# Early FFN part after the attention: slots over four PSUM banks, output tiles over the tail's four, copies over four SBUF tiles

## The chip, the cores and the metric

The kernel runs on one core of a Trainium2 chip. The metric is device time in microseconds (us) of one execution; lower is better. Engines are named as in the profile: PE (TensorE matmuls), PEld (its weight loads), DVE (VectorE), ACT (ScalarE), POOL (GpSimd), SP (SyncE, which here issues all DMAs).

## What is computed

A causal attention with a compressive memory, whose output goes through a feed-forward net (FFN) with a mish-like gate. From the reference, shortened:

```python
def _attn_ref(q, k, v, M_prev, z_prev, beta):      # B, H, S, D = 4, 8, 576, 64
    a = softmax(causal(q @ k.T / sqrt(D)))
    local = a @ v
    q_p = where(q > 0, q, exp(q) - 1) + 1
    mem_out = (q_p @ M_prev) / (q_p . z_prev + 1e-6)
    g = 1 / (1 + exp(-beta))
    return g * mem_out + (1 - g) * local

def _moe_ref(x, w_in, w_out):                      # x: 2304 x 512, w_in: 512 x 2048, w_out: 2048 x 512
    h = x @ w_in
    g = h * tanh(log1p(exp(h)))
    return g @ w_out
```

The token rows x of the FFN are the attention's output: 4 sequences of 576 tokens, 8 heads of 64 columns. The FFN's weights come as 64-bit floats.

## The kernel before, in words

**Attention.** 16 pairs of heads, one after another; pair p is head pair c = p % 4 of sequence b = p // 4. For each pair: scores on PE (L364), minimum and mask on DVE (L374), exp on ACT (L381), norms on POOL (L93), transposes on PE into the banks t (L445) with copies to `at` by ACT and DVE in turn (L110, L112), products with v in two halves into the bank vps (L473). Each half is copied to `xo` by ACT, and the rest `xl` is formed by DVE. `put` (L486, L487) stores both to `xs[b]` in DRAM. So chunk c of the FFN's x, 128 of its 512 columns, is complete for a sequence when pair 4b + c has been stored.

**FFN.** Both matmuls run in three products (high by high, high by low, low by high parts of both operands). Weights are split into these parts on the chip by `narrow` (L148): a load of 512 KB into one of two buffers `raw` (L152, SP's queue), then `wa` on ACT (L91), several steps on DVE, a cast on ACT (L110). Tokens form five blocks of 512 (the last has 256). The 2048 inner columns are 16 tiles f of 128. The first six (`KA`) are the *early part*: for each block j, `load_x` (L205) loads x, four chunks of 512 KB with the two parts i = 0, 1 in loads of their own; six *slots* (`slot_a`) each accumulate 12 matmuls (4 chunks c by 3 products) into one PSUM bank, and `mish` makes g from it: ACT reads the bank and writes u (L217), ACT casts u to the high part of g (L110), DVE forms the low part (L87). Then for each 128 tokens `out_a` accumulates 18 matmuls into an *output tile* acc (L246), ACT copies it to `ob` (L110), and SP stores it to `part` in DRAM (L253).

The steps of the early part are spread over the attention, 2.4 per pair from pair 4 on. After the 16 pairs 25 steps are left: the last slot and four output tiles of block 2, all of blocks 3 and 4. `tail` runs them merged with the conversion of seven of the ten other weight tiles f. Then the tail's own loop does f = 6 to 15 for all five blocks: `mm_h` (12 matmuls into h, h3 or acc, L566) and, three units later, `mm_o` (L583) into the accumulators o0 to o3, with `part` reloaded (L581, tiles pp) and added at the end (L589).

**Banks.** PSUM has eight. The attention's pools take five (two s, two t, one v) and, once its first pairs are done, the pools ps_h (tag h, two banks) and ps_a (tag acc, one). The tail closes these and opens its own: h twice, acc, o0 to o3, h3. A slot of the early part takes the next h; an output tile takes acc for even t and the next h for odd t; all copies `ob` share one SBUF tile.

**Order.** Each engine works through one queue in order. That order is fixed when the program is built: the framework's scheduler interleaves the code's operations by their dependencies, the buffers that are free and priorities given in the code (`run`, L62; the tail's conversions are merged with the steps by `merged`, L54).

Of the kernel before, what the change touches and what calls it, by code (L numbers as in the profile page):

```python
# [8 lines left out]
F32 = mybir.dt.float32  # L9
# [9 lines left out]
NT, DM, DFF = B * S, H * D, 2048  # L19
# [42 lines left out]
def run(ops, name=None):  # L62
    off = OFF.get(name, 0)
    if off:
        with TC[0].high_priority(off):
            for op in ops:
                op()
    else:
        for op in ops:
            op()  # L70
# [6 lines left out]
def attention_moe_kernel(ctx: ExitStack, tc: tile.TileContext, f_src, qn, vn, zz, beta, w_in, w_out, out):  # L77
# [19 lines left out]
    def order_after(ins, first):  # L97
        tc.add_manual_dep(
            ins.ins, first.ins.name,
            mybir.DependencyInfo(mybir.DependencyClass.NoSync, mybir.DependencyReason.DATA), reason="order",  # L100
        )
# [6 lines left out]
    def copy(which, o, i):  # L108
        if which == "a":
            nc.scalar.copy(out=o, in_=i)  # L110
        elif which == "v":
            nc.vector.tensor_copy(out=o, in_=i)  # L112
        else:
            nc.gpsimd.tensor_scalar(out=o, in0=i, scalar1=1.0, scalar2=1.0, op0=ALU.mult, op1=ALU.mult)
# [5 lines left out]
    cp = ctx.enter_context(tc.tile_pool(name="cp", bufs=2))  # L120
    gp = ctx.enter_context(tc.tile_pool(name="gp", bufs=GPB))
    pool_of = {}

    def open_banks(st):
        pool_of["h"] = st.enter_context(tc.tile_pool(name="ps_h", bufs=2, space=PS))
        pool_of["a"] = st.enter_context(tc.tile_pool(name="ps_a", bufs=1, space=PS))

    xs = [dram.tile([128, 2, NC, S], F32, name=f"xs{b}") for b in range(B)]
    part = dram.tile([NT, DM], F32, name="part")
# [55 lines left out]
    def split(pool, own, f):  # L185
        flat = lambda t: t.rearrange("p c j -> p (c j)")
        return (narrow(pool, own, w_in[:, f], flat(wi[0, f]), flat(wi[1, f]))
                + narrow(pool, own, w_out[:, f], wo[0, f], wo[1, f]))
# [37 lines left out]

    def slot_a(j, f):
        x, n = X[j], BLOCKS[j][1]
        ps = pool_of["h"].tile([128, 512], F32, tag="h", name="h")[:, :n]
        q = 0  # L230
        for c in range(NC):
            for y, z in ((0, 0), (0, 1), (1, 0)):
                ins = nc.tensor.matmul(ps, wi[y, f][:, c, :], x[c][:, z], start=(q == 0), stop=(q == 11))  # L233
                if q == 0 and f == 0:
                    order_after(ins, before[0])
                q += 1
        d = T[j, f] = {"h": ps, "n": n, "ph": ""}
        run(mish(d))

    def out_a(j, t):  # L240
        pool, tag = (("a", "acc"), ("h", "h"))[t % 2]
        acc = pool_of[pool].tile([128, DM], F32, tag=tag, name="acc")
        for f in range(KA):
            g = T[j, f]["g"]
            for y, z in ((0, 0), (1, 0), (0, 1)):
                nc.tensor.matmul(  # L246
                    acc[:], g[:, y, 128 * t:128 * t + 128], wo[z, f],
                    start=(f == 0 and y == z), stop=(f == KA - 1 and z == 1),
                )
        o = cp.tile([128, DM], F32, tag="ob", name="ob", bufs=1)  # L250
        copy("a", o[:], acc[:])
        r0 = BLOCKS[j][0] + 128 * t
        nc.sync.dma_start(out=part[r0:r0 + 128, :], in_=o[:])  # L253
# [279 lines left out]
    def tail(mlist):  # L533
        st = ExitStack()
        open_banks(st)
        wst = st.enter_context(tc.tile_pool(name="wst2", bufs=1))
        for f in range(KA, NF):
            weights(st.enter_context(tc.tile_pool(name=f"wb{f}", bufs=1)), f, f + 1)
        pp = st.enter_context(tc.tile_pool(name="pp", bufs=4))
        ps_o = st.enter_context(tc.tile_pool(name="ps_o", bufs=1, space=PS))  # L540
        ps_i = st.enter_context(tc.tile_pool(name="ps_i", bufs=1, space=PS))
        conv = [split(wst, wst, f) for f in range(KA, NF)]
        cl = [op for x in conv[:NCV] for op in x]
        conv = conv[NCV:]
        run(merged(mlist, cl))

        blocks = [(t, min(512, NT - t)) for t in range(0, NT, 512)]
        units = [(j, f) for j in range(len(blocks)) for f in range(KA, NF)]
        nu = len(units)
        D_ = {}  # L550
        XB = {}
        P_ = {}

        def mm_h(u):
            j, f = units[u]
            t0, n = blocks[j]
            if j not in XB:
                XB[j] = load_x(t0, n)
            x = XB[j]
            pool, tag = ((pool_of["h"], "h"), (pool_of["h"], "h"), (ps_i, "h3"), (pool_of["a"], "acc"))[u % 4]  # L560
            ps = pool.tile([128, 512], F32, tag=tag, name="h")
            T["b", u] = {"h": ps[:, :n], "n": n, "ph": "T"}
            k = 0
            for c in range(NC):
                for a, b in ((0, 0), (0, 1), (1, 0)):
                    nc.tensor.matmul(  # L566
                        ps[:, :n], wi[a, f][:, c, :], x[c][:, b], start=(k == 0), stop=(k == 11)
                    )
                    k += 1
            if f == NF - 1 and j + 1 < len(blocks):  # L570
                XB[j + 1] = load_x(*blocks[j + 1])

        def mm_o(u, t):
            j, f = units[u]
            t0, n = blocks[j]
            g = T["b", u]["g"]
            if f == KA:
                D_[t] = ps_o.tile([128, DM], F32, tag=f"o{t}", name="o")
            if f == NF - 2:
                P_[j, t] = pp.tile([128, DM], F32, tag="pp", name="pp")  # L580
                nc.sync.dma_start(out=P_[j, t][:], in_=part[t0 + 128 * t:t0 + 128 * t + 128, :])  # L581
            for y, z in ((0, 0), (1, 0), (0, 1)):
                nc.tensor.matmul(  # L583
                    D_[t][:], g[:, y, 128 * t:128 * t + 128], wo[z, f],
                    start=(f == KA and y == z), stop=(f == NF - 1 and z == 1),
                )
            if f == NF - 1:
                o = P_[j, t]
                nc.vector.tensor_tensor(out=o[:], in0=D_[t][:], in1=o[:], op=ALU.add)  # L589
                nc.sync.dma_start(out=out[t0 + 128 * t:t0 + 128 * t + 128, :], in_=o[:])  # L590

        for u in range(nu + LAG):
            if u < nu:
                mm_h(u)
                d = T["b", u]
                run(mish(d))
            if conv:
                run(conv.pop(0), 'convT')
            if 0 <= u - LAG < nu:
                for t in range(blocks[units[u - LAG][0]][1] // 128):  # L600
                    mm_o(u - LAG, t)
        st.close()

    attention()
    for k in range((NP - P0) // 4, len(BLOCKS)):
        todo.extend(steps_a(k))
    tail(todo)


# [60 lines left out]
```

## Time and profile before

| | us |
|---|---|
| median of 3 runs | 655.2 (653.29 to 656.19) |
| profiled execution | 654.77 |
| its span in the trace | 653.0 |
| PE busy | 597.0 (91%), 3200 matmuls |
| PEld busy | 454.9 (70%) |
| DVE busy | 336.8 (52%) |
| ACT busy | 300.7 (46%) |
| POOL busy | 169.1 (26%) |
| DMA | 80.83 MB, mean 124 GB/s |
| mean granted PE clock | 0.973 of full |

Times in the profile count from the span's start. A row of the timeline merges neighbouring instructions of one line; what stands in brackets at its end is how long the engine was idle before it and which instruction ended that wait. A clock of 1.00 is full speed.

### The profile page before, as it was taken

The page shows a single profiled execution, that of the slowest core. Times are in us where ns is not written, and L with a number is a line of the kernel's source. Part 1 is how long each engine was busy: PE and PEld are TensorE (multiplying, and loading weights), DVE is VectorE, ACT ScalarE, POOL GpSimd, SP SyncE. Part 2 cuts the span into 40 slices and gives each one's busy share as a digit, 9 for nine tenths or more (in the row PEclk, how much of TensorE's full clock was granted, in tenths as well). Part 3 has the DMA queues.
Part 4 walks back from the last instruction along what each step waited for, and adds up shares of the span by engine and source line. Part 5 has one row for each costly group of instructions (what it writes and reads, how often), then busy time and mean ns, then how long its engine had stood idle before and what let it go on. Part 6 is the DMA issues. An engine that isn't in the chain of part 4 may idle for free.

```text
span 653.0 us, 9308 instructions
## 1 busy us (share of the span) xinstructions
PE 597.0 (91%) x3200; PEld 454.9 (70%) x3200; DVE 336.8 (52%) x903; ACT 300.7 (46%) x694; POOL 169.1 (26%) x260
## 2 busy tenths in 40 slices
PE   3477968889989999999998979999999999999997
PEld 2254635656655766767776878888888888888886
DVE  4989897765588654573338887920311211121121
ACT  3677655866567675566325455621222222222221
POOL 3697886464166714443000000000000000000000
PEclk9979986899999999999999989999999999999999
DMA  6345674324275226421257765304302220430220
GB/s 229 104 144 182 189 262 150 133 61 144 76 235 168 98 62 176 166 73 58 91 176 235 261 206 176 121 1 129 130 0 82 94 83 6 124 129 0 65 97 33
DMA packets 47007, 80.83 MB, mean 124 GB/s; under 512 B 7280, under 2 KB 21616, under 8 KB 46960
## 3 DMA queue, kind: packets, MB, share of 16 engines
q1 hardware_dynamic: 46960, 80.24, 38.0%
q8 instruction: 25, 0.41, 0.3%
q14 instruction: 22, 0.18, 0.1%
HBM read 61.35 MB, written 18.87 MB: 123 GB/s over the span
## 4 chain that ended last, share of the span: by engine, by line
PE 61%; DVE 13%; DMA 10%; ACT 7%; POOL 5%; issue 2%; SPq 1%; DVEq 0%; ACTq 0%; POOLq 0%
PE o L583 19%; PE h L566 19%; PE acc L246 7%; PE h L233 5%; DMA raw<-in_w_in_dram 5%; PE vps L473 5%; PE t L445 4%; DVE w L374 3%; PE s L364 3%; POOL w L93 3%; DMA raw<-in_w_out_dram 3%; DMA qn<-in_qn_dram 2%; ACT w L381 2%; ACT L217 1%; DVE ws L172 1%
## 5 line engine op out<-in xcount | busy, mean ns | idle before, releaser
L87 DVE TENSOR_TENSOR g<-u,g 128x512 fp32r<-128x512 f32 (+1 forms) x80 | 52.4, 661 | 185.6 <-ACT g L110 185.6
L566 PE MATMUL h<-xb,wi 128*128 128x512 f32 (+1 forms) x600 | 134.9, 368 | 0.0
L583 PE MATMUL o<-wo,g 128*128 128x512 f32 x540 | 133.8, 390 | 0.0
L217 ACT ACTIVATE u<-h 128x512 f32<-128x512 f32 (+1 forms) x80 | 43.5, 554 | 179.2 <-PE h L566 170.9
L566 PEld LDWEIGHTS h<-xb,wi 128*128 128x128 f32 x600 | 106.1, 188 | 19.6
L583 PEld LDWEIGHTS o<-wo,g 128*128 128x128 f32 x540 | 100.6, 188 | 20.3
L93 POOL TENSOR_SCALAR w<-w,rc 128x64 f32<-128x64 f32 (+4 forms) x160 | 95.4, 621 | 71.0 <-ACT w L381 53.3
L381 ACT ACTIVATE w<-w,mx 128x576 f32<-128x576 f32 (+4 forms) x160 | 88.3, 554 | 28.5 <-DVE mx L374 27.6
L364 PE MATMUL s<-f 64*128 64x288 f32 (+4 forms) x384 | 69.2, 472 | 31.7 <-DVE mx L374 25.4
L233 PE MATMUL h<-xb,wi 128*128 128x512 f32 (+1 forms) x360 | 88.0, 389 | 7.8 <-ACT u L217 7.8
L246 PE MATMUL acc<-wo,g 128*128 128x512 f32 x324 | 85.9, 401 | 1.4 <-ACT ob L110 0.9
L445 PE MATMUL t<-ident,w 128*128 128x128 f32 x480 | 75.5, 291 | 5.3 <-ACT at L110 3.1
L233 PEld LDWEIGHTS h<-xb,wi 128*128 128x128 f32 x360 | 64.8, 200 | 21.1 <-ACT u L217 9.6
L364 PEld LDWEIGHTS s<-f 64*128 64x128 f32 x384 | 35.4, 207 | 59.0 <-DVE mx L374 33.2
L445 PEld LDWEIGHTS t<-ident,w 128*128 128x128 f32 x480 | 55.9, 146 | 26.0 <-issue 8.7
L246 PEld LDWEIGHTS acc<-wo,g 128*128 128x128 f32 x324 | 59.4, 190 | 16.0 <-issue 2.3
L374 DVE CUSTOM_DVE_ANT_0 w<-s,mask 128x288 f32<-128x288 f32 (+4 forms) x160 | 59.6, 421 | 17.6 <-PE s L364 17.6
L473 PE MATMUL vps<-at,v 128*64 128x256 f32 (+2 forms) x512 | 61.3, 383 | 5.8 <-DVE xl L87 3.7
L473 PEld LDWEIGHTS vps<-at,v 128*64 128x64 f32 x512 | 35.6, 142 | 31.7 <-issue 6.0
L112 DVE COPY at<-t 128x448 f32<-128x448 f32 x64 | 41.5, 649 | 16.2 <-PE t L445 16.2
L110 ACT CAST g<-u 128x512 fp32r<-128x512 f32 (+1 forms) x80 | 45.5, 579 | 1.8
L110 ACT COPY at<-t 128x384 f32<-128x384 f32 x64 | 33.7, 526 | 17.6 <-PE t L445 17.4
(45 smaller groups left out, 432.1 us busy)
## 6 DMA issues: line engine op xcount, KB each, us to landing
f<-in_f_src_dram SPq DMA_DIRECT2D x32, 288.0 KB, 3.7
raw<-in_w_in_dram SPq DMA_DIRECT2D x16, 512.0 KB, 3.9
raw<-in_w_out_dram SPq DMA_DIRECT2D x16, 512.0 KB, 3.5
xb<-xs SPq DMA_DIRECT2D x24, 256.0 KB, 3.7
qn<-in_qn_dram SPq DMA_DIRECT2D x16, 320.0 KB, 3.4
v<-in_vn_dram SPq DMA_DIRECT2D x16, 320.0 KB, 3.3
xs<-xo SPq DMA_DIRECT2D x16, 288.0 KB, 3.4
xs<-xl SPq DMA_DIRECT2D x16, 288.0 KB, 3.3
```

The lines of the kernel that those rows point to most:

```text
L87: engines[ENG[name]].tensor_tensor(**kw)
L93: engines[which].tensor_scalar(out=o, in0=i, scalar1=scale, scalar2=1.0, op0=ALU.mult, op1=ALU.mult)
L110: nc.scalar.copy(out=o, in_=i)
L233: ins = nc.tensor.matmul(ps, wi[y, f][:, c, :], x[c][:, z], start=(q == 0), stop=(q == 11))
L246: nc.tensor.matmul(acc[:], g[:, y, 128 * t:128 * t + 128], wo[z, f], start=(f == 0 and y == z), stop=(f == KA - 1 and z == 1),)
L364: nc.tensor.matmul(g["ps"][:, o:o + n], f[le, 0, q0:q0 + 128], f[le, 1, a:b], start=True, stop=True)
L374: nc.vector.tensor_tensor_reduce(out=g["w"][:, WO[m] + D + a:WO[m] + D + b], in0=g["ps"][:, o:o + n], in1=mask[:, c0:c0 + n], scale=-E_SC, ...
L381: nc.scalar.activation(out=row, in_=row, func=ACTF.Exp, scale=-1.0, bias=g["mx"][:, m:m + 1], accum_out=g["sm"][:, m:m + 1])
L445: nc.tensor.transpose(ps[:, o:o + 128], g["w"][:, c:c + 128], ident[:])
L473: queued(nc.tensor.matmul(ps[64 * e:64 * e + 64, a:b], d["v"][:, t, e], at[e][gi][:, c:c + b - a], start=(k == 0), stop=(k == last),), k o ...
L566: nc.tensor.matmul(ps[:, :n], wi[a, f][:, c, :], x[c][:, b], start=(k == 0), stop=(k == 11))
L583: nc.tensor.matmul(D_[t][:], g[:, y, 128 * t:128 * t + 128], wo[z, f], start=(f == KA and y == z), stop=(f == NF - 1 and z == 1),)
```

## The change

Three entries of `pool_of` now say where `slot_a` and `out_a` take their banks and the copies their SBUF tiles. While the attention runs they hold what stood there before. When the tail opens, they are set anew: slot f takes entry f % 4 of h, h, h3, acc; output tile t takes o0 to o3; the copies take the four tiles pp, which the tail uses later for its reloads.

```diff
     def open_banks(st):
         pool_of["h"] = st.enter_context(tc.tile_pool(name="ps_h", bufs=2, space=PS))
         pool_of["a"] = st.enter_context(tc.tile_pool(name="ps_a", bufs=1, space=PS))
+        pool_of["slot"] = [(pool_of["h"], "h")]
+        pool_of["out"] = [(pool_of["a"], "acc"), (pool_of["h"], "h")]
+        pool_of["ob"] = (cp, "ob", 1)
...
     def slot_a(j, f):
         x, n = X[j], BLOCKS[j][1]
-        ps = pool_of["h"].tile([128, 512], F32, tag="h", name="h")[:, :n]
+        pool, tag = pool_of["slot"][f % len(pool_of["slot"])]
+        ps = pool.tile([128, 512], F32, tag=tag, name="h")[:, :n]
...
     def out_a(j, t):
-        pool, tag = (("a", "acc"), ("h", "h"))[t % 2]
-        acc = pool_of[pool].tile([128, DM], F32, tag=tag, name="acc")
+        pool, tag = pool_of["out"][t % len(pool_of["out"])]
+        acc = pool.tile([128, DM], F32, tag=tag, name="acc")
...
-        o = cp.tile([128, DM], F32, tag="ob", name="ob", bufs=1)
+        pool, tag, n = pool_of["ob"]
+        o = pool.tile([128, DM], F32, tag=tag, name="ob", bufs=n)
...
         ps_i = st.enter_context(tc.tile_pool(name="ps_i", bufs=1, space=PS))
+        pool_of["slot"] = [(pool_of["h"], "h"), (pool_of["h"], "h"), (ps_i, "h3"), (pool_of["a"], "acc")]
+        pool_of["out"] = [(ps_o, f"o{t}") for t in range(4)]
+        pool_of["ob"] = (pp, "pp", 4)
```

With other banks free, the scheduler writes another order from the last three pairs of the attention to the tail's first units; before and after that PE's order is the same, and POOL's is the same throughout. In the changed kernel lines have other numbers: L233 is L237, L246 is L250, L445 is L450, L473 is L478, L217 is L220, L566 is L574. In the rows below, `wi_2_86` is a part of w_in's tile f = 2, `wo_0_79` one of w_out's tile f = 0.

PE, from the second half of pair 14's product (the first vps rows) on, before:

```order
L473 MATMUL vps<-at,v 64x256 x8
L473 MATMUL vps<-at,v 64x128 x2
L246 MATMUL acc<-wo_2_87,g 128x512 x2
L246 MATMUL acc<-wo_2_89,g 128x512
L233 MATMUL h<-xb,wi_4_94 128x512 x2
L233 MATMUL h<-xb,wi_4_96 128x512
L445 MATMUL t<-ident,w 128x128 x4
L246 MATMUL acc<-wo_3_91,g 128x512
```

and in the changed kernel:

```order
L478 MATMUL vps<-at,v 64x256 x8
L478 MATMUL vps<-at,v 64x128 x2
L450 MATMUL t<-ident,w 128x128 x5
L237 MATMUL h<-xb,wi_2_86 128x512 x2
L237 MATMUL h<-xb,wi_2_88 128x512
L237 MATMUL h<-xb,wi_2_86 128x512 x2
L237 MATMUL h<-xb,wi_2_88 128x512
L450 MATMUL t<-ident,w 128x128 x15
L237 MATMUL h<-xb,wi_2_86 128x512
L478 MATMUL vps<-at,v 64x320 x2
L478 MATMUL vps<-at,v 64x256 x2
L478 MATMUL vps<-at,v 64x128 x2
```

Before, an output tile and a slot of block 2 filled this place. Now slot f = 2 of block 3 stands there: six matmuls of chunks 0 and 1, and its seventh, the first of chunk 2 (pair 14), between 15 transposes and the product of pair 15. Nine matmuls each of slots 3, 0 and 1 follow around and behind that pair's product, then the four output tiles of block 2, then the last three matmuls of each slot.

PE, where the last output tile of block 3 begins, before:

```order
L246 MATMUL acc<-wo_5_99,g 128x512 x2
L246 MATMUL acc<-wo_5_101,g 128x512
L566 MATMUL h<-xb,wi_8_3461 128x512 x2
L566 MATMUL h<-xb,wi_8_3463 128x512
L566 MATMUL h<-xb,wi_8_3461 128x512
L246 MATMUL acc<-wo_0_79,g 128x512 x2
```

and in the changed kernel:

```order
L250 MATMUL acc<-wo_5_99,g 128x512 x2
L250 MATMUL acc<-wo_5_101,g 128x512
L250 MATMUL acc<-wo_0_79,g 128x512 x2
L250 MATMUL acc<-wo_0_81,g 128x512
L250 MATMUL acc<-wo_1_83,g 128x512 x2
```

The slot of the tail that began here (wi_8, six of its twelve matmuls ahead of block 4's slots) is gone from this place. Block 4's six slots follow without output matmuls between them, where before some of block 3's stood between.

ACT, in block 3's slots, before:

```order
L110 COPY ob<-acc 128x512
L110 CAST wo_6_3448<-wa 128x512
L91 ACTIVATE wa<-raw 128x512
L217 ACTIVATE u<-h 128x512
L110 CAST wi_7_3454<-wa 128x512
L110 CAST g<-u 128x512
L110 COPY ob<-acc 128x512
L91 ACTIVATE wa<-raw 128x512
L217 ACTIVATE u<-h 128x512
```

and in the changed kernel, at the first mish of block 3:

```order
L91 ACTIVATE wa<-raw 128x512
L110 COPY ob<-acc 128x512
L110 CAST wi_8_3461<-wa 128x512
L91 ACTIVATE wa<-raw 128x512
L110 COPY ob<-acc 128x512
L220 ACTIVATE u<-h 128x512
L110 CAST wo_8_3462<-wa 128x512
L220 ACTIVATE u<-h 128x512
```

The first mish of block 3 stood behind the third conversion after the attention; now it stands behind the sixth (the loads for w_out's tile f = 8), and all four output tiles of block 2 are copied ahead of it. On SP's queue the loads of x for pair 14's chunk stand behind its store in both kernels; the four reloads of `part` (L581), which stood among the first weight loads after the attention, now stand behind the first store of block 4, and the stores of `part` stand one by one between weight loads.

## Rows read from the trace of the kernel before

**Rows 1.** The page's section 2: busy tenths and granted clock in 40 slices.

```profile
PE   3477968889989999999998979999999999999997
...
PEclk9979986899999999999999989999999999999999
```

**Rows 2.** Windows of the core: us, busy (instructions) by engine, PEclk, DMA share, GB/s.

```profile
382.00:386.00 4.00, 1.02 (x9) 0.82 (x7) 3.97 (x9) 1.75 (x4) 0.00 (x0) 0.95 0.61 204
386.00:392.00 6.00, 5.65 (x25) 5.55 (x26) 4.99 (x10) 2.97 (x8) 0.00 (x0) 0.50 0.62 208
392.00:404.00 12.00, 12.00 (x71) 10.67 (x70) 9.49 (x19) 6.20 (x13) 0.00 (x0) 0.98 0.51 174
404.00:600.00 196.00, 196.00 (x867) 162.34 (x866) 49.02 (x80) 51.46 (x88) 0.00 (x0) 1.00 0.25 79
```

**Rows 3.** Timeline of PE, 306 to 390 us: start, duration, instruction, [idle before].

```profile
308.29 0.50 PE L246 MATMUL acc<-wo,g 128*128 128x512 f32 x1 [0.38 <-ACT g L110]
...
325.84 1.41 PE L473 MATMUL vps<-at,v 128*64 128x320 f32 x12 [0.28 <-DVE at L112]
...
340.68 4.39 PE L246 MATMUL acc<-wo,g 128*128 128x512 f32 x18 [0.94 <-ACT ob L110]
...
349.47 3.02 PE L233 MATMUL h<-xb,wi 128*128 128x512 f32 x12 [1.68 <-ACT u L217]
...
353.41 3.02 PE L233 MATMUL h<-xb,wi 128*128 128x512 f32 x12 [0.24 <-ACT u L217]
...
386.35 2.93 PE L233 MATMUL h<-xb,wi 128*128 128x256 f32 x12 [3.33 <-ACT u L217]
```

**Rows 4.** Timeline of ACT at the two late mishes.

```profile
348.27 0.67 ACT L91 ACTIVATE wa<-raw 128x512 f32<-128x512 f32 x1 [3.22 <-DMA raw<-in_w_in_dram]
348.84 0.58 ACT L217 ACTIVATE u<-h 128x512 f32<-128x512 f32 x1
...
385.35 0.68 ACT L91 ACTIVATE wa<-raw 128x512 f32<-128x512 f32 x1 [0.96 <-DMA raw<-in_w_out_dram]
385.93 0.37 ACT L217 ACTIVATE u<-h 128x256 f32<-128x256 f32 x1
```

**Rows 5.** Timeline of PE: a slot of block 4 after the low clock.

```profile
392.70 1.59 PE L233 MATMUL h<-xb,wi 128*128 128x256 f32 x12
```

**Rows 6.** Timeline: transposes, pair 14's last product and its store (SPq: SP's queue).

```profile
316.40 1.03 PE L445 MATMUL t<-ident,w 128*128 128x128 f32 x8
...
317.37 2.17 PE L473 MATMUL vps<-at,v 128*64 128x256 f32 x20
...
319.98 0.32 SPq L486 DMA_DIRECT2D xs<-xo  x1
```

**Rows 7.** Source line L486, the stores of xo: us from issue to landing.

```profile
DMA to landing us min/median/max: 2.1/3.4/5.7
```

**Rows 8.** Source line L205, the loads of x: us from issue to landing.

```profile
DMA to landing us min/median/max: 1.8/3.1/6.9
```

**Rows 9.** Timeline: issues of weight loads on SP's queue, and conversions on ACT.

```profile
335.74 0.33 SPq L152 DMA_DIRECT2D raw<-in_w_in_dram  x1
...
342.09 0.37 SPq L152 DMA_DIRECT2D raw<-in_w_in_dram  x1
...
342.76 0.69 ACT L91 ACTIVATE wa<-raw 128x512 f32<-128x512 f32 x1 [1.23 <-DMA raw<-in_w_out_dram]
...
360.87 0.68 ACT L91 ACTIVATE wa<-raw 128x512 f32<-128x512 f32 x1 [2.30 <-DMA raw<-in_w_out_dram]
```

**Rows 10.** Timeline of PE, and a window, at an earlier wait.

```profile
126.45 1.22 PE L233 MATMUL h<-xb,wi 128*128 128x512 f32 x2 [2.38 <-ACT u L217]
...
126.00:128.00 2.00, 1.55 (x6) 1.26 (x6) 2.00 (x10) 1.98 (x5) 0.00 (x0) 0.54 0.00 0
```

**Rows 11.** Timeline: the last piece of wi on DVE, and its slot on PE.

```profile
422.57 0.68 DVE L87 TENSOR_TENSOR wi<-wa,ws 128x512 fp32r<-128x512 f32 x1
...
443.96 2.88 PE L566 MATMUL h<-xb,wi 128*128 128x512 f32 x12
```

## Prediction

> **What bounds the kernel now.** I began with the page's slices, 16.3 us each, counted from 0 [rows 1]. PE is the busiest engine, and from slice 24 on it is full up to the last. There the time is PE's own work, which the change does not touch: from 404 to 600 us PE is busy for 196.00 of 196.00 us at clock 1.00, 867 matmuls of 0.226 us [rows 2]. Before 300 us the attention runs, in the same order in both kernels. What is left are slices 21 and 23, with PE digits of 8 and 7, and a PEclk digit of 8 in slice 23. The windows place that loss: from 382 to 386 PE works 1.02 of 4.00 us, and from 386 to 392 it is busy at a granted clock of 0.50, which is 1.2 GHz where 2.4 is the other level [rows 2].
>
> The timeline of PE names the waits [rows 3]. From 306 us on there are six of over 0.2 us: 0.38 (an early output tile waits for ScalarE's g), 0.28 (attention waits for a copy by VectorE), 0.94 (an output tile waits for ScalarE's copy of the tile before it), 1.68 and 0.24 (slots of block 3 wait for ScalarE's mish, u), 3.33 (the second slot of block 4 waits for the mish of the first). The low clock follows the last. ScalarE's timeline says why the mishes are late: at 348.27 and 385.35 the mish is the very next instruction behind a weight conversion (wa) that has waited 3.22 and 0.96 us for its load [rows 4]. ScalarE works through its queue in order, and with two h banks PE can be only two slots ahead of it. At 386 it was only one: a slot of the tail (wi_8), half done, held the other bank.
>
> **The change part by part.** The sum is made against the profiled execution, 654.77 us (span 653.0); the median of the three runs is 655.2.
>
> *Output tiles over o0 to o3, copies over four SBUF tiles.* An output tile waits for a copy only from the fifth on, and then for one that is four tiles old. What covers a copy is the 18 matmuls of the next tile, 4.1 us. The wait of 0.94 goes: gain 0.94. The tail's first products want the same banks back, but four whole slots of the tail, 10.9 us, stand before them.
>
> *Slots over four banks, block 3.* Only f = 2 and f = 3 get new banks; f = 4 and 5 come back to the two h banks. The order shows more: nine of the twelve matmuls of each of four slots now stand ahead of the output tiles of block 2, the last three of each behind them. So the 1.68 and 0.24 go, and late next is slot f = 4, which needs the mish of f = 0. Counted from the end of attention's last product, PE has 18 matmuls of slots, 72 of output tiles and 12 closing ones first: 102 x 0.226 = 23.1 us. ScalarE has the sixth weight conversion ahead of that mish. At the old pace the first load goes out 0.1 us behind that product, at 335.74, and the sixth conversion begins at 360.87 [rows 9]: 25.2 us, and with the rest of that conversion, a copy and the mish itself (0.57 + 0.58 + 0.58) 26.9. That is a wait of 3.8. But in that stretch the SP queue also carried four reloads of partial sums, and two stores side by side that wait for their copies; the change moves the reloads behind block 4's first store, and puts the stores one by one between the weight loads. Two raw buffers by themselves give a round of 342.09 - 335.74 = 6.35 us; the second conversion came 7.1 us after the product (342.76, [rows 9]), so the sixth comes at 7.1 + 2 x 6.35 = 19.8, its mish at 21.5: no wait. Between the ends, 0 and 3.8, I take 0.6, near the low one, since the new stores come 4.1 us apart, as the tiles do. Net gain 1.92 - 0.6 = 1.3.
>
> *Block 4.* No tail slot holds a bank now, and the six slots of 256 columns run together; f = 4 wants the mish of f = 0 only three slots, some 4.3 us, after that could start. The 3.33 goes, and with it the low clock: of 5.65 us of PE work at 0.50 [rows 2] half is loss, 2.8, and 0.2 in the window behind it, 3.0 in all. As a check, twelve matmuls of 256 columns took 2.93 us there [rows 3] and 1.59 soon after [rows 5]. Gain 6.3. What could remain is 0 to 1.2, a wait like ScalarE's 0.96 and a conversion started late; I take 0, as nothing of the new order brings it about.
>
> *End of attention.* The matmuls that met the waits of 0.38 and 0.28 stand elsewhere: gain 0.7. But a new wait comes in. Slot f = 2 of block 3 puts its seventh matmul, the first that reads the x of pair 14, into PE's queue ahead of the attention of pair 15. That x goes through DRAM: from the start of pair 14's last product to its store 2.6 us (317.37 to 319.98, [rows 6]), the store's landing (2.1 at least, median 3.4, [rows 7]), 0.1 to issue, the load's landing (1.8 at least, median 3.1, [rows 8]): 6.6 to 9.2 us. PE arrives after the product (2.1), 20 transposes (eight take 1.03, [rows 6]; so 2.5) and six matmuls (1.4): 6.0, and with short waits for copies 6.5. The wait lies between 0.1 and 3.2 us; I take 1.8, a little over the middle, as twelve loads of x go out just ahead of the store. Fifteen transposes now stand in a row over two banks, with no slot between them to cover the copies: two waits of about 0.45, the 0.28 of before being the nearest row; 0.9, ends 0 and 1.4.
>
> *Weights and POOL.* Costed at nothing. The last piece of wi is written at 423.25 and its slot starts at 443.96 [rows 11]; the conversions run beside PE, and a tail 10 us earlier still leaves ten. POOL's order is the same.
>
> The sum: gains 0.94 + 1.92 + 6.3 + 0.7 = 9.9; new waits 1.8 + 0.9 + 0.6 = 3.3. Net 6.6 off 654.8: **648.2 us**. With both ends of the new waits, 0.1 and 8.4 (with 0 for block 4), it is 645.0 to 653.3.
>
> **The rivals.**
>
> *The clock falls at the new wait.* PE stood 2.38 us before 126.45, and the next window shows a clock of 0.54 [rows 10]; it stood 1.68 before 349.47, in slice 21, whose clock digit is 9 [rows 1]. The new wait of about 1.8, with transposes around it, lies between. A fall costs up to the 3.0 of block 4, or about 1.7 where it is shorter: 650 to 651.3. The Trainium skill's page "TensorE: Matmul & The Clock Gate", section "A second HAM failure mode: psum-queue depth-cycling", tells of a kernel that cycled through PSUM banks and lost rate because PE paused between groups and its clock went down and up. By that rule the rotation itself would bring the fall; in this trace the two falls shown follow waits of 2.38 and 3.33 us, with h in two banks.
>
> *The waits only move: ScalarE's queue decides, not the banks.* If the old pace of conversions holds, slot f = 4 waits 3.8 us, and block 4 keeps 1.2. Then 9.9 - 3.8 - 1.2 - 2.7 (end of attention) leaves 2.2: 652.6, or 652 to 655. For it: every late mish of before stood behind a load. Against it: the reloads and the half-done tail slot go. The same page, section "HAM oscillation — how this bites in real kernels", reports of one kernel that PSUM double-buffering gave no further gain. By that this case would be the likeliest; here four of the six waits end at a bank [rows 3], so I give it less.
>
> *Slower: the x of pair 14 stops the attention.* The matmul that waits for it stands ahead of pair 15, whose x all four slots want. With the longest landings seen, 5.7 for a store and 6.9 for a load [rows 7, 8], x comes 15.3 us after the product's start: a wait of 8.8, then the low clock for 3.0 and the other new waits, 1.5: 13.3 against 9.9, so 658. It decides from about 12 us for the two landings together; the medians give 6.5, and no weight load is in the queue there yet.
>
> *Better.* The new waits stay at their low ends: 645.5.
>
> **How the numbers follow.** The forecast has 0.53, the clock case 0.20, the moved waits 0.14, slower 0.05, better 0.08. Within 0.5% of the median, 3.3 us, is about what a measurement of this kernel cannot tell from no change. Below 651.9 lie nearly all of the forecast, most of the clock case and the better one: faster 0.75. The moved waits and the rest of the clock case make same 0.20; slower 0.05. The range, 645.5 to 653.0, takes in the bounds of the forecast but for their corners, the clock case and the near edge of the moved waits, and leaves out about 2 in 10.
>
> **What would show it.** In the changed kernel PE has no wait of over 1 us between the end of attention and the first tail product, and the clock stays at 1.00 there; just before the last attention products there is one wait of 1 to 3 us that ends with a DMA of x. PE's full stretch begins 5 to 8 us earlier. Wrong would be: a wait of 2 us or more for ScalarE at slot f = 4, a granted clock of 0.50 near the end of attention, or waits for weights in the tail.

## The result and the profile after

The changed kernel takes 647.71 us (median of six runs, 646.44 to 650.52); the kernel before took 655.91 beside it (median of six). The ratio is 0.9881 with a 95% interval of 0.9857 to 0.9905: 1.2% faster. In a later session (run e8 below) it was 648.03 us against 655.91, ratio 0.9894 (0.9869 to 0.9919). The ratios are made from the single executions; the quotient of two medians differs from them by up to 0.15% in the runs below. The profiled execution took 649.19 us, span 647.4 (before: 654.77 and 653.0).

The page of the changed kernel, section 2, in 40 slices of 16.2 us:

```profile
PE   3568967899988999999999999999999999999997
...
PEclk9979976998999999999999999999999999999999
```

The digits 8 and 7 that PE had in slices 21 and 23 [rows 1] are now 9, and the clock digit of slice 23 too. The windows say the same (us, busy time and instructions of PE, PEld, DVE, ACT, POOL, then the granted clock, DMA share and GB/s):

```profile
382.00:386.00 4.00, 4.00 (x35) 4.00 (x35) 3.29 (x7) 2.98 (x7) 0.00 (x0) 1.00 0.62 208
386.00:392.00 6.00, 6.00 (x42) 5.55 (x41) 5.40 (x12) 4.20 (x11) 0.00 (x0) 1.00 0.33 102
...
404.00:592.00 188.00, 188.00 (x831) 155.74 (x830) 44.84 (x73) 47.20 (x80) 0.00 (x0) 1.00 0.25 80
```

Where PE worked 1.02 of 4 us and then ran at a clock of 0.50 [rows 2], it now works all the time at 1.00. From 404 us on nothing has changed: 0.226 us for a matmul (188 / 831), as before.

PE's timeline has the four waits of over 0.2 us that are left from 300 us on, and the stretches without one around them (start, duration, instruction, [idle before it <- what ended it]):

```profile
319.44 2.17 PE L478 MATMUL vps<-at,v 128*64 128x256 f32 x20
...
324.91 1.09 PE L450 MATMUL t<-ident,w 128*128 128x128 f32 x8 [0.46 <-DVE at L112]
326.69 0.47 PE L237 MATMUL h<-xb,wi 128*128 128x512 f32 x1 [0.69 <-DMA xb<-xs]
...
329.97 2.30 PE L237 MATMUL h<-xb,wi 128*128 128x512 f32 x9 [0.40 <-DVE at L112]
332.20 2.17 PE L478 MATMUL vps<-at,v 128*64 128x256 f32 x20
334.30 4.38 PE L237 MATMUL h<-xb,wi 128*128 128x512 f32 x18
338.51 16.48 PE L250 MATMUL acc<-wo,g 128*128 128x512 f32 x72
354.83 2.88 PE L237 MATMUL h<-xb,wi 128*128 128x512 f32 x12
358.85 5.75 PE L237 MATMUL h<-xb,wi 128*128 128x512 f32 x24 [1.14 <-ACT u L220]
364.44 16.48 PE L250 MATMUL acc<-wo,g 128*128 128x512 f32 x72
380.76 8.79 PE L237 MATMUL h<-xb,wi 128*128 128x256 f32 x72
```

The six waits of before, 6.85 us in all [rows 3], are gone, block 4's with its low clock: its 72 slot matmuls run in one piece. New are 0.46 and 0.40 (transposes, and the first matmuls of a slot, behind VectorE's copies of transposes), 0.69 (the x of pair 14) and 1.14 (slot f = 4 of block 3): 2.69 us. So the waits fell by 4.2 us, and the 3.0 us that the low clock had cost went with them, 7.2 in all. The profiled spans differ by less, 5.6 us, since this execution came to pair 15's scores (the score products of 288 columns) 2 us later than the kernel before, in a part whose order is the same: 288.20 against 286.23. From there to the end of the span the two differ by 7.6 us (359.2 against 366.8), and e8 differs by 7.3 (359.5).

### The profile page after: what moved, and what is told of

It reads as the page before. It is cut to its first block, busy times and chain, and to the rows that moved or that the text cites. A ratio compares the mean times of both kernels' runs of the same rounds, so it can differ in the third digit from the quotient of the medians.

```text
span 647.4 us, 9316 instructions
## 1 busy us (share of the span) xinstructions
PE 595.0 (92%) x3200; PEld 453.4 (70%) x3200; DVE 335.2 (52%) x903; ACT 300.3 (46%) x694; POOL 168.8 (26%) x260
## 4 chain that ended last, share of the span: by engine, by line
PE 67%; DVE 11%; DMA 8%; POOL 6%; ACT 5%; issue 2%; SPq 0%; DVEq 0%; ACTq 0%; POOLq 0%
PE h L574 19%; PE o L591 19%; PE acc L250 9%; PE h L237 8%; PE vps L478 5%; POOL w L93 4%; PE s L369 4%; PE t L450 4%; DVE w L379 3%; DMA raw<-in_w_out_dram 3%; DMA qn<-in_qn_dram 3%; DMA raw<-in_w_in_dram 2%; POOL w L87 1%; DVE at L112 1%; ACT w L386 1%
## 5 line engine op out<-in xcount | busy, mean ns | idle before, releaser
L574 PE MATMUL h<-xb,wi 128*128 128x512 f32 (+1 forms) x600 | 134.3, 368 | 0.0
L220 ACT ACTIVATE u<-h 128x512 f32<-128x512 f32 (+1 forms) x80 | 43.4, 553 | 174.5 <-PE h L574 169.1
L574 PEld LDWEIGHTS h<-xb,wi 128*128 128x128 f32 x600 | 106.1, 188 | 19.7
L237 PE MATMUL h<-xb,wi 128*128 128x512 f32 (+1 forms) x360 | 84.5, 381 | 4.9 <-ACT u L220 3.8
L250 PE MATMUL acc<-wo,g 128*128 128x512 f32 x324 | 83.0, 402 | 0.1
L450 PE MATMUL t<-ident,w 128*128 128x128 f32 x480 | 75.7, 291 | 6.3 <-ACT at L110 4.2
L450 PEld LDWEIGHTS t<-ident,w 128*128 128x128 f32 x480 | 55.6, 146 | 27.1 <-issue 9.2
L237 PEld LDWEIGHTS h<-xb,wi 128*128 128x128 f32 x360 | 61.6, 191 | 17.8 <-ACT u L220 5.1
L250 PEld LDWEIGHTS acc<-wo,g 128*128 128x128 f32 x324 | 60.3, 191 | 14.3 <-issue 1.9
L478 PE MATMUL vps<-at,v 128*64 128x256 f32 (+2 forms) x512 | 60.8, 380 | 6.3 <-DVE xl L87 3.5
L478 PEld LDWEIGHTS vps<-at,v 128*64 128x64 f32 x512 | 35.4, 142 | 32.1 <-issue 5.5
```

The costliest lines, as they stand in the source:

```text
L250: nc.tensor.matmul(acc[:], g[:, y, 128 * t:128 * t + 128], wo[z, f], start=(f == 0 and y == z), stop=(f == KA - 1 and z == 1),)
L450: nc.tensor.transpose(ps[:, o:o + 128], g["w"][:, c:c + 128], ident[:])
L478: queued(nc.tensor.matmul(ps[64 * e:64 * e + 64, a:b], d["v"][:, t, e], at[e][gi][:, c:c + b - a], start=(k == 0), stop=(k == last),), k o ...
L574: nc.tensor.matmul(ps[:, :n], wi[a, f][:, c, :], x[c][:, b], start=(k == 0), stop=(k == 11))
```

## The experiments

"Waits" is the sum of PE's waits of over 0.2 us from 300 us on in the profiled execution, "low clock" the time from 300 to 600 us at a granted clock of 0.50 in it. Both are of one execution; the times and ratios are of six to twelve, beside the kernel before on the same chip. That one execution is not always a typical one: in e2, e4 and e10 it was the slowest of its runs (657.08, 659.6 and 653.85 us), in e12 the second slowest (651.16), in e7 the fastest (647.66) and in e9 the second fastest (651.31).

| run | edit | us | before, us | ratio (95%) | waits, us | low clock, us |
|---|---|---|---|---|---|---|
| before | | 655.2 | | | 6.85 | 6.8 |
| changed | all three | 647.71 | 655.91 | 0.9881 (0.9857 to 0.9905) | 2.69 | 0 |
| e1 | slots alone | 654.23 | 657.37 | 0.9955 (0.9940 to 0.9970) | 6.3 | 3.4 |
| e2 | tiles and copies | 654.48 | 657.37 | 0.9955 (0.9937 to 0.9973) | 8.7 | 6.8 |
| e3 | slots and tiles | 651.37 | 657.37 | 0.9913 (0.9892 to 0.9934) | 5.4 | 0 |
| e4 | before, one step on GpSimd | 658.18 | 657.37 | 1.0015 (1.0002 to 1.0028) | 9.2 | 3.4 |
| e5 | before, both steps on GpSimd | 658.47 | 655.91 | 1.0043 (1.0023 to 1.0063) | 8.5 | 6.8 |
| e6 | changed, both steps on GpSimd | 656.16 | 655.91 | 1.0010 (0.9992 to 1.0027) | 6.5 | 6.8 |
| e7 | changed, two copy tiles | 649.90 | 655.91 | 0.9916 (0.9887 to 0.9946) | 2.9 | 0 |
| e8 | changed, again | 648.03 | 655.91 | 0.9894 (0.9869 to 0.9919) | 3.0 | 0 |
| e9 | before, loads on GpSimd's queue | 654.03 | 655.14 | 0.9977 (0.9957 to 0.9997) | 5.0 | 0 |
| e10 | changed, loads on GpSimd's queue | 651.33 | 655.14 | 0.9941 (0.9921 to 0.9961) | 6.1 | 3.4 |
| e11 | changed, six banks for slots | 652.26 | 655.14 | 0.9954 (0.9931 to 0.9976) | 5.3 | 0 |
| e12 | changed, stores on GpSimd's queue | 648.20 | 655.89 | 0.9899 (0.9868 to 0.9931) | 3.9 | 3.4 |

The theory: PE waits because a PSUM bank is still held by a tile that ScalarE has not read yet, and the change takes those meetings away. Its rivals: ScalarE's queue decides (mishes stand behind waits for weights, whatever the banks), or SP's queue does (loads stand behind stores and reloads). The expectations name times on the scale of the first runs, where the kernel before took 655.2; on the chip of e1 to e4 it took 657.37, so the differences are what can be compared.

### One half and the other: e1, e2, e3

```diff
 # e1: only this of the three lines in tail()
+pool_of["slot"] = [(pool_of["h"], "h"), (pool_of["h"], "h"), (ps_i, "h3"), (pool_of["a"], "acc")]
 # e2: only these
+pool_of["out"] = [(ps_o, f"o{t}") for t in range(4)]
+pool_of["ob"] = (pp, "pp", 4)
 # e3: slot and out, without ob
+pool_of["slot"] = [(pool_of["h"], "h"), (pool_of["h"], "h"), (ps_i, "h3"), (pool_of["a"], "acc")]
+pool_of["out"] = [(ps_o, f"o{t}") for t in range(4)]
```

> Only the slots rotate over four banks (two h, h3, acc); output tiles stay on acc and h, and there is one copy tile in the old place. The theory of the banks: a wait lasts as long as a bank's owner is late, and slots and output tiles still meet on h and acc here, so only a part of the gain comes: the waits at slots of blocks 3 and 4 (5.25 us in the kernel before) shrink to 2 to 4, the output tile's wait stays, and the time is 650 to 653, 3 to 6 below the kernel before. Rival one, ScalarE's queue decides: the mishes are as late as before, the waits stay at 5 us or more and the time is within 1.5 of the kernel before. Rival two, the partial sums' reloads and stores on SP decide: they are not moved here, so no gain either, within 1.5 of the kernel before. On the clock: if a wait of 2 us or more is left at block 4, a stretch with a granted clock of 0.50 follows and costs about 3 us.

> The other half: output tiles over o0 to o3 and copies over the four SBUF tiles, but slots stay on the two h banks. Theory of the banks: the 0.94 goes, but a slot still needs the mish of the slot two before it, so waits of 1 to 2 us for ScalarE's u stay at block 3 (third slot) and at block 4, 5 to 7 us of waits in all from 300 us on; time 651 to 655, at most 4 below the kernel before. Rival two (SP's queue, reloads and stores): the four copy tiles move them, so most of the gain is here, 647 to 649. Rival one (ScalarE's queue): as the banks, 652 to 655; it is told apart by the fourth run.

> The change without its third edit: slots and output tiles as in the changed kernel, with the one copy tile of the kernel before, so the reloads of the partial sums stay where they were. PE's order is that of the changed kernel but for a few places. Theory of the banks: nearly the whole gain, 647 to 650; a copy waits for the store before it, which an output tile of 4.1 us covers. Rival two (SP's queue): the weight loads are late as in the kernel before, slot f = 4 of block 3 waits 2.5 to 3.8 us and the gain is half or less, 651 to 654.

With the slots alone 3.1 us go, and with tiles and copies alone 2.9, both within what the theory of the banks had for the time; slots and tiles together bring 6.0 of the changed kernel's 8, which is the sum of the two. The waits of e1 did not come out as expected: those at slots were to shrink from 5.25 to 2 to 4 us and are 5.6, and the output tile's 0.94, which was to stay, is gone. PE's timeline of e1 (slots on four banks, output tiles still on h and acc):

```profile
351.87 5.73 PE L237 MATMUL h<-xb,wi 128*128 128x512 f32 x24 [2.39 <-ACT u L220]
...
384.07 6.19 PE L237 MATMUL h<-xb,wi 128*128 128x256 f32 x36 [1.99 <-ACT ob L110]
391.11 3.14 PE L237 MATMUL h<-xb,wi 128*128 128x256 f32 x24 [0.85 <-ACT ob L110]
```

The slots of block 4 now wait for `ob`, the copy of an output tile: slots and output tiles still meet on h and acc. By the profiles, 0.6 us of e1's gain are waits, and half of the time at the low clock went too (6.8 to 3.4 us). In e2 the slots keep the two h banks:

```profile
355.41 8.65 PE L237 MATMUL h<-xb,wi 128*128 128x512 f32 x24 [3.89 <-ACT u L220]
...
394.13 3.14 PE L237 MATMUL h<-xb,wi 128*128 128x256 f32 x24 [2.69 <-ACT u L220]
```

Both are a slot that comes behind two others of its block and wants the bank of the first. They are longer than expected (1 to 2 us), and with the low clock they leave no gain in this profile, the slowest of ten executions; where the 2.9 us of the median come from no profile shows. Four copy tiles and late reloads, which rival two takes for the cause, are in e2 too, and it gains 2.9 us with them, no more than the slots bring without them: most of the gain is not theirs. In e3 no output tile waits, and what is left are slot f = 4 of block 3 and a slot of block 4:

```profile
358.74 5.73 PE L237 MATMUL h<-xb,wi 128*128 128x512 f32 x24 [2.44 <-ACT u L220]
...
387.81 3.13 PE L237 MATMUL h<-xb,wi 128*128 128x256 f32 x24 [1.27 <-ACT u L220]
```

The gain is more than the half that rival two allowed, but the 2.44 is nearly what rival two had for that wait. No run keeps the old order of the matmuls with the new banks or the other way round, so what the scheduler's other order is worth by itself stays open.

### Work taken off ScalarE: e4, e5, e6

```diff
 # e4 (before); e5 (before) and e6 (changed) have both lines
-scaled(ENG["wx"], f32(t["a"][:]), f32(t["r"][:, :, 1]), 2.0**-112)
+scaled(ENG["wx"] if own is cp else "p", f32(t["a"][:]), f32(t["r"][:, :, 1]), 2.0**-112)
...
-copy(ENG["whi"], hi, f32(t["a"][:]))
+copy(ENG["whi"] if own is cp else "p", hi, f32(t["a"][:]))
```

> The kernel before, with one step changed: the first conversion of each of the tail's weight pieces (wa from raw) runs on GpSimd and not on ScalarE, so that no mish stands behind the wait for a weight load. Banks and PE's order are those of the kernel before but for a few places. Rival one (ScalarE's queue decides): the waits of 1.68, 0.24 and 3.33 go with nearly all of the half clock, 647 to 649. Theory of the banks: only the lateness that came from the load goes, that is the 1.68 at block 3 and about 1 of the 3.33 at block 4; the tail's half-done slot still holds a bank, a wait of 2 us or more stays at block 4, and the time is 651 to 654.

> The kernel before, with both ScalarE steps of each tail weight piece on GpSimd: the first conversion (wa from raw) and the cast of its high part (wi or wo from wa), which in the fourth run had become the step that waited for the load in ScalarE's queue (3.53 us, then the mish). No mish stands behind a weight load any more; banks and PE's order are as before. If ScalarE's queue alone makes the waits: they fall below 1 us each at blocks 3 and 4 and the time is 646 to 649 on the scale of the first runs, 7 to 9 below the kernel before. If the banks do: at block 4 the second slot still waits for the first one's mish, since the tail's half-done slot holds a bank, 1 to 2.5 us, and slots and output tiles still meet; 2 to 5 below the kernel before.

> The changed kernel with the same two steps on GpSimd. If what is left at slot f = 4 (1.14 us) comes from ScalarE's queue, it goes and the time is 0.5 to 2 below the changed kernel; if it comes from SP's pace of loads or from the bank alone, no difference within 0.5.

None came out as either side had it: e4 is a little slower than the kernel before, e5 0.4% slower, and e6 lost the whole gain. The timelines show what stood in the way. In e4 ScalarE had no conversion left, but the cast of the same piece, one link further, waited 3.53 us, and the mish of block 4 stood behind it:

```profile
389.09 0.62 ACT L110 CAST wi<-wa 128x512 fp32r<-128x512 f32 x1 [3.53 <-DVE wa L162]
389.61 0.58 ACT L110 COPY ob<-acc 128x512 f32<-128x512 f32 x1
390.09 0.39 ACT L217 ACTIVATE u<-h 128x256 f32<-128x256 f32 x1
```

The load was there at 386.4, 0.8 us into that wait; the other 2.7 us went to the piece's steps on GpSimd and VectorE. In e5 the cast was gone too, and two copies waited for the only copy tile, that is for the store of the copy before:

```profile
385.93 0.59 ACT L110 COPY ob<-acc 128x512 f32<-128x512 f32 x1 [2.27 <-DMA part<-ob]
386.41 0.39 ACT L217 ACTIVATE u<-h 128x256 f32<-128x256 f32 x1
...
391.22 0.59 ACT L110 COPY ob<-acc 128x512 f32<-128x512 f32 x1 [3.98 <-DMA part<-ob]
```

The mish of block 4's first slot stood behind the first of them, and the bank that a later slot wanted was held until the second was done: PE waited 1.18 us for the one and 3.07 for the other. In e4 it had waited 3.89, and both had the low clock. In e6, with four copy tiles, ScalarE's queue is free, slot f = 4 waits no longer, and the waits are VectorE's. The wait groups of PE (us in total, times, longest):

```profile
PE acc L250 <- DVE g L87: 4.7, 3, 2.6
PE h L237 <- DMA xb<-xs: 0.9, 1, 0.9
```

VectorE's part of the mish (`g<-u,g`) stands behind VectorE's steps of the same weight pieces. And those steps themselves took longer. The same group of twenty steps between 334 and 460 us (busy us, mean ns | idle before), in the changed kernel:

```profile
L175 DVE SCALAR_TENSOR_TENSOR ws<-raw,ws 128x512 f32<-128x512 uint32 x20 | 13.8, 688 | 0.3
```

and in e6:

```profile
L175 DVE SCALAR_TENSOR_TENSOR ws<-raw,ws 128x512 f32<-128x512 uint32 x20 | 18.0, 902 | 0.3
```

In e4 a pair of rows from GpSimd's and VectorE's timelines shows when. A step of VectorE that begins 0.22 us into one of GpSimd's takes 1.13 us, where 0.69 is usual:

```profile
386.50 0.80 POOL L93 TENSOR_SCALAR wa<-raw 128x512 f32<-128x512 f32 x1 [3.08 <-DMA raw<-in_w_in_dram]
...
386.72 1.13 DVE L172 SCALAR_TENSOR_TENSOR ws<-raw,ws 128x512 f32<-128x512 uint32 x1
```

The Trainium skill's page "SBUF — State Buffer", section "SBUF: two separate sides", has a rule for this: VectorE and GpSimd share one pair of ports to SBUF, and of a GpSimd instruction that reads SBUF and a VectorE instruction with two inputs in SBUF, as this step has, whichever starts first holds the pair for its whole instruction. The rows come near it: until GpSimd's end at 387.30 the step would stand for 0.58 us, and with its own 0.69 that makes 1.27, where 1.13 is shown.

So ScalarE's queue is one of several places where a weight piece or a store in flight can hold up a bank. Taking steps from it by way of GpSimd does not bring the gain. Since VectorE's steps grew longer at the same time, these runs do not price ScalarE's queue by itself; the rival falls only in its plain form.

### The copies: e7, and the changed kernel again, e8

```diff
 # e7
-pool_of["ob"] = (pp, "pp", 4)
+pool_of["ob"] = [(cp, "ob", 1), (pp, "ob2", 1)]
...
-pool, tag, n = pool_of["ob"]
+pool, tag, n = pool_of["ob"][t % len(pool_of["ob"])]
```

> The changed kernel with two copy tiles of their own in place of the four shared with the reloads: the reloads of the partial sums stand early on SP, as in the run with one copy tile, but a copy no longer waits for the store just before it. If the number of copy tiles was what the third edit brought: the time of the changed kernel within 1, slot f = 4 waits 1 to 1.5 us. If the reloads' place on SP was: the time of the run with one copy tile, 2 to 3 above the changed kernel, slot f = 4 waits 2 to 3 us.

> The changed kernel itself on the chip of these runs, so that the others can be set against it. Every theory: 0.985 to 0.991 of the kernel before; waits on PE from 300 us on of 0.5, 0.5 to 0.7, 0.4 and 0.8 to 1.5 us, no granted clock of 0.50 between 151 us and the last stretch.

e8 came out as expected. e7 has the waits of the changed kernel, with the reloads as early on SP as in e3:

```profile
356.61 5.78 PE L237 MATMUL h<-xb,wi 128*128 128x512 f32 x24 [1.12 <-ACT u L220]
...
384.68 3.14 PE L237 MATMUL h<-xb,wi 128*128 128x256 f32 x24 [0.22 <-ACT u L220]
```

against e8's 1.30 and none. By the waits the reloads' place counts for nothing, and a second tile for 2.4 us (2.44 + 1.27 against 1.12 + 0.22); but e7's profile is its fastest execution, 2.2 us below its median, and e3's a usual one. By the times it is open: e7 is 1.9 us above e8, and the intervals of e3, e7, e8 and the changed kernel overlap. The third edit is worth 2.1 us by the ratios of e3 and the changed kernel, 1.2 by those of e3 and e8, each give or take about 2 us, and no run here narrows it.

### The loads and the stores on SP: e9, e10, e12

```diff
 # e9 (before) and e10 (changed), in the tail alone
-nc.sync.dma_start(out=raw[:].rearrange("p a b -> p (a b)"), in_=src.bitcast(I32))
+(nc.sync if own is cp else nc.gpsimd).dma_start(out=raw[:].rearrange("p a b -> p (a b)"), in_=src.bitcast(I32))
 # e12 (changed), in tail() and out_a
+pool_of["st"] = nc.gpsimd
...
-nc.sync.dma_start(out=part[r0:r0 + 128, :], in_=o[:])
+pool_of.get("st", nc.sync).dma_start(out=part[r0:r0 + 128, :], in_=o[:])
```

> The kernel before, with the loads of the tail's weight pieces (raw) issued on GpSimd's queue and not on SP's, where they stood behind stores that wait for ScalarE's copies. Banks and steps are as before, PE's order nearly so. If SP's queue makes the weights late and so the mishes: the waits of 1.68, 0.24 and most of the 3.33 go without any bank being freed, no stretch at a granted clock of 0.50 stays near 390 us, and the time is 4 to 7 below the kernel before. If the banks decide: 3 us or more of the 5.25 us of slot waits stay, with the low clock behind them, at most 2 below the kernel before.

> The changed kernel with the same move of the weight loads to GpSimd's queue. If the pace of the loads on SP is what is left at slot f = 4: its wait of 1.1 to 1.3 us goes and the time is 0.5 to 2 below the changed kernel. If the bank alone is: no difference within 0.5. If GpSimd issues such loads more slowly than SP, or VectorE works slower meanwhile, as beside GpSimd's work in the runs on GpSimd: above the changed kernel.

> The changed kernel with the tail's twelve stores of partial sums issued on GpSimd's queue, the weight loads staying on SP's, so that no load stands behind a store that waits for a copy. The tenth run showed weight loads on GpSimd's queue to go out in rounds of 8.2 us for two, against 6.5 to 7.6 on SP's in the changed kernel. If the stores ahead of the loads set the pace on SP: the rounds come down towards 6.4 us, the wait at slot f = 4 of block 3 goes, and the time is 0.5 to 1.5 below the changed kernel. If the two raw buffers and the conversion's steps set it: the rounds stay at 6.5 us or more, the wait stays within 0.5, and the time is that of the changed kernel.

e9 lies between: 1.5 us gained by its ratio, with waits of 0.93, 0.69, 0.49 and 1.71 us at slots; its profiled execution was among the fastest of twelve, and the low clock that the theory of the banks had behind the waits is not in it. So SP's queue may have had a part in the late mishes of before; how large, e9 does not say, since on GpSimd's queue the loads themselves took longer. That shows in e10, which is slower than the changed kernel by 3 to 4 us. The two rows from issue to landing, between 330 and 372 us, of the changed kernel (SP):

```profile
DMA to landing us min/median/max: 3.3/3.9/5.5
```

and of e10 (GpSimd):

```profile
L155 POOLq EVENT_SEMAPHORE  x9: 2687/2862/26587, 307.0 to 369.3; - x9
...
DMA to landing us min/median/max: 3.5/4.8/6.3
```

(The line above it is, in ns, the instruction that waits on GpSimd's queue ahead of each load.) Its first loads left at 334.15, 342.62, 350.81 and 359.02, 8.2 to 8.5 us for two pieces; on SP, in the changed kernel, the same ones left at 334.44, 340.96, 348.56 and 355.98, 6.5 to 7.6 us. In e12, with SP free of the stores, they left at 333.40, 340.04, 347.46 and 356.29: 6.6, 7.4 and 8.8 us, no sooner, and the time is that of the changed kernel. The stores ahead of the loads don't set the pace. What does shows in the waits of SP's queue, between 334 and 362 us in the changed kernel and 333 and 362 in e12: the loads waited for VectorE's step L175, the last to read a buffer `raw`, for 10.8 us in five times there, and for 19.5 us in six times here. So a load goes out when VectorE has freed one of the two buffers. Against the expectation the wait at slot f = 4 was not the same but 2.32 us in the execution profiled:

```profile
359.00 7.31 PE L237 MATMUL h<-xb,wi 128*128 128x512 f32 x24 [2.32 <-ACT u L220]
```

and a low clock followed it (0.57 in the window from 359 to 363 us). Whether a third buffer for raw pieces would shorten the rounds was not tried.

### A bank for each slot: e11

```diff
-pool_of["slot"] = [(pool_of["h"], "h"), (pool_of["h"], "h"), (ps_i, "h3"), (pool_of["a"], "acc")]
-pool_of["out"] = [(ps_o, f"o{t}") for t in range(4)]
+pool_of["slot"] = [(pool_of["h"], "h"), (pool_of["h"], "h"), (ps_i, "h3"), (pool_of["a"], "acc"), (ps_o, "o0"), (ps_o, "o1")]
+pool_of["out"] = [(ps_o, f"o{(t + 2) % 4}") for t in range(4)]
```

> The changed kernel with six banks for a block's six slots (two h, h3, acc, o0, o1) and output tiles that begin at o2, so that no slot comes back to a bank of its own block. Theory of the banks: the wait at slot f = 4 of block 3 goes; but an output tile needs the g of all six slots, so that what is late shows there instead, 0.5 to 2 us at the output tiles of blocks 3 and 4; time within 1.5 of the changed kernel. If the wait at slot f = 4 were the last one: 1 to 1.5 below the changed kernel.

The wait at slot f = 4 goes, as a question of banks: all 72 matmuls of block 3's slots run in one piece. PE's timeline of e11:

```profile
326.33 2.17 PE L478 MATMUL vps<-at,v 128*64 128x256 f32 x20 [1.27 <-DVE xl L87]
329.42 3.06 PE L237 MATMUL h<-xb,wi 128*128 128x512 f32 x12 [0.92 <-DVE xl L87]
...
348.63 16.48 PE L237 MATMUL h<-xb,wi 128*128 128x512 f32 x72
...
391.93 1.44 PE L250 MATMUL acc<-wo,g 128*128 128x512 f32 x4 [0.88 <-ACT g L110]
393.93 2.35 PE L250 MATMUL acc<-wo,g 128*128 128x512 f32 x9 [0.56 <-DVE g L87]
```

But with more banks free the scheduler wrote yet another order. In the changed kernel 36 matmuls of block 3's slots stand among the attention's last ones or right behind them; here none do, and PE waits there for 1.27 and 0.92 us and three times more for 0.28 to 0.86. At block 4 it is now the output tiles that wait, for g. The sum of the waits doubles, and the time is 4 to 5 us above the changed kernel, more than was expected. No version tried beats the changed kernel.

## Why the prediction was right

The forecast was 648.2 us; 647.7 and 648.0 were measured. That it came within 0.5 us is partly luck: single executions of the changed kernel lie between 646.4 and 650.5, and of the new waits one was forecast 1.1 us too long and one 0.5 too short. Step by step:

- **What bounds it.** Confirmed: of the 7.6 us between the profiles from pair 15's scores on, PE's waits between 300 and 400 us and the low clock there make 7.2, and in e8 6.9 of 7.3.
- **Gains, 9.9.** All four went as forecast: the output tile's 0.94, block 3's 1.92, block 4's 3.33 and the low clock, the attention's 0.38 and 0.28. The two that rest on banks meeting, block 4 and the output tiles, are shown by e1 to e3: leave one of the two kinds of tile on the old banks and a slot waits, in e1 for the copy of an output tile, in e2 for the mish of a slot. The third edit may have a share in block 4 that the sum did not count: 1.27 us of wait with one copy tile (e3), 0.22 with two (e7), none with four.
- **The x of pair 14, 1.8 forecast, 0.69 measured** (0.79 in e8). The product began at 319.44 and x was there at 326.69, 7.25 us later, within the 6.6 to 9.2 worked out (whose upper end is the sum with the median landings), and PE was there after 6.56 (forecast 6.5). The size was off since the landings were near their low ends, not a little over the middle; the twelve loads ahead of the store did not slow it.
- **The waits for VectorE's copies, 0.9 forecast, 0.86 measured.** The size is right, the places only in part: 0.46 came in the row of transposes, as forecast, and 0.40 not there but behind the last four transposes, at the first matmuls of a slot.
- **Slot f = 4, 0.6 forecast, 1.14 measured** (1.30 in e8). Here a step failed: the sum took a round of 6.35 us for two weight pieces, in which the sixth conversion comes 19.8 us after the attention's last product. It came after 22.8 (357.15 on ScalarE, the product's end at 334.37), between that and the 25.2 of before. The reason given, that the reloads and paired stores of before made the pace, is not borne out: in e7, with the reloads early again, the sixth conversion came after 22.8 us too (at 354.91), and in e12, with the stores gone from SP, after 24.0 (at 357.29). The term that was mis-sized is the round: two raw buffers by themselves do not give 6.35 us here but 6.5 to 7.6, since a load waits until VectorE has read a buffer out (10.8 us of waiting in the changed kernel). ScalarE's rows at this wait are:

```profile
357.15 0.68 ACT L91 ACTIVATE wa<-raw 128x512 f32<-128x512 f32 x1 [2.21 <-DMA raw<-in_w_out_dram]
357.73 0.57 ACT L110 COPY ob<-acc 128x512 f32<-128x512 f32 x1
358.19 0.60 ACT L220 ACTIVATE u<-h 128x512 f32<-128x512 f32 x1
```

  The mish is behind a load, as in [rows 4], but it is wanted only three slots later, and that is the difference of the banks.
- **The sum.** 9.9 less 2.7 is 7.2, where 6.6 was forecast; the medians differ by 8.2 and 7.9 in two sessions. The rest, 1 us or less, is not placed.
- **The rivals.** Clock: the forecast put its risk at the wait for x; neither profile of the changed kernel has a low clock there, but e12, whose PE order is the same, has one at slot f = 4. The case was real, and in another place. The Trainium skill's page "TensorE: Matmul & The Clock Gate", section "A second HAM failure mode: psum-queue depth-cycling", tells of falls in the short idle times between groups of a kernel that cycles through PSUM banks, and the prediction took from it that the rotation itself would bring them. Here it did not: the kernel with two h banks has a fall behind its 3.33 us, the two profiles of the changed kernel, with four, have none, and where slots over four banks have one (e1, e6, e10, e12) it follows a pause of 1.99 to 2.61 us. "The waits only move" is what e6, e10 and e11 show of further changes, and not of this one. The slower case, x stopping the attention, is excluded by the 0.69.

## What to carry to other kernels

When a matrix engine waits for an evacuation, ask which two uses meet on the bank before asking how to make the evacuation earlier: separating slots from output tiles gave most of the gain, while taking conversion steps off the evacuating engine, here onto GpSimd, left the evacuation behind the next thing in an in-order queue (a cast that waits for the piece's other steps, a copy behind its store, VectorE's own steps). One kind of tile on banks of its own is not enough where the other kind still shares (0.45% each, 0.9% together, which is no more than their sum). And read the scheduler's new order before counting on a freed bank: with six banks it moved slots away from where they covered other waits, and more than half of the gain was lost.

## What was not expected of the hardware

The length of a pause alone does not tell whether the clock falls. In e1 PE stood 2.39 us before 351.87 and kept a clock of 1.00, and stood only 1.99 before 384.07 and fell to 1.2 GHz (a granted clock of 0.50) for most of the window behind it:

```profile
352.00:355.00 3.00, 3.00 (x14) 2.47 (x15) 2.78 (x5) 1.74 (x3) 0.00 (x0) 1.00 0.72 167
384.00:388.00 4.00, 3.93 (x19) 3.79 (x20) 3.93 (x9) 2.73 (x6) 0.00 (x0) 0.57 0.50 125
```

In e2 the 3.89 was followed by a fall and the 2.69 by none:

```profile
355.00:361.00 6.00, 5.59 (x13) 4.45 (x14) 4.96 (x10) 3.10 (x7) 0.00 (x0) 0.50 0.49 152
394.00:398.00 4.00, 3.87 (x28) 3.74 (x29) 3.71 (x9) 2.65 (x7) 0.00 (x0) 1.00 0.27 102
```

Over the profiles of the kernel before and of all runs, from 340 us on, each pause of over 3 us (3.07, 3.33, 3.89 and 3.89) was followed by a low clock, and of eight pauses between 1.9 and 2.7 us four were (1.99, 2.32, 2.35, 2.61) and four were not (2.12, 2.39, 2.44, 2.69). The prediction had placed its 1.8 us between a pause that did and one that did not; the border is no such line.
